# Attention and two MoE layers in one kernel: fewer weights decoded in the first block, zeros stored later, a steeper decode in the second MoE, two steps in another order

## The chip, the core and the metric

The kernel runs on one core of a Trainium2 chip. The metric is the device time of one execution in microseconds (us); lower is better. A core has TensorE (PE, with its weight loads PEld), VectorE (DVE), ScalarE (ACT), GpSimd (POOL) and SyncE (SP). SP computes nothing here: it issues nearly all DMAs of the kernel, in program order, and an instruction of SP that waits holds back every transfer that is written after it.

## The reference

Attention over 4 batches, 8 heads, 576 positions and 64 channels, with a causal mask and a bias that is made from running sums of `s`; then two MoE layers over all 2304 tokens, the second fed with the first one's output.

```
s_pos = np.maximum(s, 0.0)
cum = np.cumsum(s_pos, axis=-1)
bias = -(cum[:, :, :, None] - cum[:, :, None, :])
scores = np.where(causal, -1000000000.0, scores + np.minimum(bias, 0.0))
...
h = np.maximum(x @ w_in, 0.0)           # first MoE
return (h * h @ w_out).astype(np.float32)
...
h = x @ w_in                            # second MoE
g = h * np.cos(h)
return (g @ w_out).astype(np.float32)
```

## The kernel before, in words

**Blocks and jobs.** The 2304 tokens are cut into nine blocks of 256. Attention is computed in jobs: a job is one tile of up to 128 queries of one head. The first 16 heads (numbers 0 to 15, EARLY) are short ones: their keys and queries come by a plain load into a tile `early`, a few heads ahead (`load_raw`), and their scores are turned on PE (line 612). Later heads take `raw` tiles, which ACT and DVE split into `hi` and `k2` (`prep_high`, `prep_low`), and four extra rows that POOL loads from the DRAM table `ext_d`; their scores are turned by DMA transposes that SP issues (line 619).

**Steps.** `step` writes out one step of everything, in program order for each engine: parts of several jobs at different stages (mask, exponential, split, product with v), some slots of the first MoE, and some weights to decode. Each engine runs its own part in that order. A step without MoE slots belongs to the prologue: 21 steps that compute the attention of block 0. Then, for each block k, `moe_slot` hands out the slots of block k's MoE: `g1` (line 943, 12 matmuls that multiply one group f of 128 hidden channels out, for f from 0 to 15) and `g2` (line 972, 12 matmuls back), while the steps go on with the attention of block k+1. The stretch in which block 0's MoE is computed is called block 0 below; it has 17 steps, numbered here 0 to 16, each with about two slots.

**Weights.** The weights come packed as int64 bit patterns of doubles, in 32 pieces of 128x512 for each MoE; piece 2f belongs to `g1` of group f, piece 2f+1 to `g2`. A piece is loaded (`w_load`, line 190, 512 KB), clipped on ACT (`w_clip`, line 805), has its bits put together on DVE in two instructions (`w_bits`, lines 811 and 815), gets its high part from ACT (`w_hi`, line 824) and its low part from DVE (`w_lo`, line 836), and then is a matmul operand. Bits are done in one step, the high and low part in the step after it. How many pieces a step takes comes from constants: with x = step - 4, a prologue step takes int((x+1)*PROLOG_BITS) - int(x*PROLOG_BITS) pieces (PROLOG_BITS is 0.75), a step i of block 0 takes int((i+1)*1.5) - int(i*1.5), until all 32 are done. `w_need` guarantees before each slot that the pieces it uses have been written out; the wait itself is a semaphore on PE. All nine blocks reuse the decoded pieces.

**Other queues.** Work that has no place in a step stands in the list `later`, with the number of a step from which it may go; one entry is taken per step. Among them: `store_ones` at 8 (two DMAs that fill `ext_d` with ones and minus ones), `store_zeros` at 9 (four DMAs of 4x4x64 that put zeros over a part of what the ones filled, for the heads that share a tile, called paired), `pair_mask` at 10 (two small ACT copies), `store_c` at 11. A `store_ext` per unit of eight heads comes 10 jobs ahead of that unit. At the end of a step, `v_late` (the late half of v's preparation, whose last part stores a split v to DRAM, line 480) stands ahead of `heads_ahead(i, (nraw, load_raw, 4))` (the load of a coming head, lines 227 and 232).

**The second MoE.** After the ninth block, 80 steps of three groups p = 0, 1, 2 (`GROUPS`), five token blocks j (four of 512 tokens and a last one of 256, whose steps are half as long on PE) and the groups f. A step is `m2_g1` (line 1372) and, two steps later, `m2_g2` (line 1427). Its weights are decoded in the same way with a scale on top; the number decoded by step i is `goal`, line 1489.

Of the kernel before, what the change touches and what calls it, by code (L numbers as in the profile page):

```python
# [8 lines left out]
F32 = mybir.dt.float32  # L9
# [9 lines left out]
B, H, S, D = 4, 8, 576, 64  # L19
# [4 lines left out]
NF = DFF // 128  # L24
BT = 256
# [66 lines left out]
KQ = 832  # L92


def _paired(head):

    return head[4] == [64]
# [4 lines left out]
    return 128 if _paired(head) else head[6]  # L102

WAHEAD = 8
PROLOG_BITS = 0.75

EARLY = 16
FIRST_BITS = 4
B8_BITS = 0.75
P_BITS = 0.75  # L110
QUIET = 3
PAUSE = 14
# [3 lines left out]
EXT_AHEAD = 10  # L116
# [10 lines left out]
def attention_moe_moe_kernel(  # L127
# [18 lines left out]
    nc = tc.nc  # L146
    ctx.enter_context(tc.manual_schedule())
    heads = _units()
# [15 lines left out]
    ext_d = dram.tile([len(heads), 4, KQ], F32, name="ext_d")  # L164
# [6 lines left out]
    mask = const.tile([128, 768], BF16, name="mask")  # L171
# [26 lines left out]
    one = wp.tile([128, 1024], F32, tag=f"w{2 * NF - 7}", name="one")  # L198
# [36 lines left out]
    def v_own(b):  # L235
# [24 lines left out]
        out=ident, in_=ident, pattern=[[-1, 128]], compare_op=ALU.not_equal, fill=1.0,  # L260
# [23 lines left out]
    def store_ones(eng, n0, n1):  # L284
# [10 lines left out]
        out=mask[:, 384:512], in_=mask[:, 384:512], pattern=[[-1, 128]], compare_op=ALU.is_ge,  # L295
        fill=-8.0e9, base=0, channel_multiplier=1,
    )
    for t in early[2:]:
        early_ones(t, nc.gpsimd)
    nc.vector.tensor_scalar(  # L300
        out=cs[0:32, 0:S], in0=cs[0:32, 0:S], scalar1=0.0, scalar2=8.0, op0=ALU.max, op1=ALU.mult
    )
    cc = []
    for x0, x1, t in ((0, BT, "xh"), (BT, S, "xl")):
        nc.vector.tensor_tensor_scan(
            out=c8[0:32, x0:x1], data0=cs[0:32, x0:x1], data1=cs[0:32, x0:x1],
# [8 lines left out]
    for r in range(2):  # L315
        nc.gpsimd.memset(one[0:len(heads), BT * r:BT + (KQ - BT) * r], 1.0 - 2.0 * r)

    nc.gpsimd.memset(one[0:H // 2, KQ:KQ + 64], 0.0)

    def pair_mask():  # L320
        for r in (0, 64):
            nc.scalar.copy(mask[r:r + 64, 704:768], mask[0:64, 384:448])

    def store_zeros():
        for n in range(EARLY, len(heads), H):
            for x in range(2 if _paired(heads[n]) else 0):
                nc.sync.dma_start(
                    out=ext_d[n + x:n + H:2, :, BT - 64 - 64 * x:BT - 64 * x],
                    in_=one[0:H // 2, None, KQ:KQ + 64].to_broadcast([H // 2, 4, 64]),
                )  # L330

    def split_sums(x0, x1, t):
        c = m1.tile([128, KD * BT], F32R, tag=t, bufs=2, name="cc")
# [5 lines left out]
    def store_ext(n):  # L339
        u, b, h, q0, rws, o, nq, nk, nl = heads[n]  # L340
        src = c_d[b * H:(b + 1) * H]
        nc.sync.dma_start(out=ext_d[n:n + H, 0:2, BT:BT + nl], in_=src[:, :, 0:nl])
        if _paired(heads[n]):
            for x in range(2):
                e = ext_d[n + x:n + H:2]
                nc.sync.dma_start(out=e[:, 2:4, BT - 128 + 64 * x:BT - 64 + 64 * x], in_=src[x::2, :, q0:q0 + nq])
            return
        nc.sync.dma_start(out=ext_d[n:n + H, 2:4, BT - nq:BT], in_=src[:, :, q0:q0 + nq])

# [145 lines left out]
    def v_late():  # L495
        if vq:
            for f, g in vq.pop(0):
                if f not in (v_scale, v_sum):
                    f(g)
# [270 lines left out]
    def job(i):  # L770
        return jobs[i] if 0 <= i < NJ else None
# [7 lines left out]
    def heads_ahead(i, *fs):  # L779
        if job(i) and jobs[i][1] == 0:  # L780
            for cnt, f, d in fs:
                upto(cnt, jobs[i][0] + d, f)

    def unit_done(u):
        return last_job[u] + lag(last_job[u]) + 3
# [197 lines left out]
    def y_store():  # L983
        while yst:
            k, a, st = yst.pop(0)
            nc.sync.dma_start(out=y_d[k, :, 2 * a:2 * a + 2, :], in_=st)
# [59 lines left out]
    seg0 = [n for n in range(NH) if heads[n][2] == 0]  # L1046
    later = []
# [53 lines left out]
    def step(moe=0, bits=0, attn=True):  # L1101

        i = prog[0]
        held = len(xtq)
        prog[0] += attn
        if attn:
            for j in stage(1, i - 2):
                emit_exp(j)
        x_high()
        if attn and job(i - 2):  # L1110
            emit_turn(i - 2)
        if attn:
            heads_ahead(i, (next_, load_ext, 2))
        w_age()
        w_scales()
        n = moe_slot() if moe else None
        slow = bool(vq) and any(f is v_wait for f, g in vq[0])
        if slow:
            v_sums()
        if attn:  # L1120
            heads_ahead(i, (nhigh, prep_high, 2))
        _weave(evacuate())
        y_evict()
        if not attn or g2done[0] < 2:
            rests()
        if xcq and xcq[-1][-1] and xcq[-1][0] == 1:
            x_low()
        _weave(softmax_tail(i) if attn else None, w_step(bits), None if slow else v_early())
        x_low()
        rests()  # L1130
        w_lows()
        if attn and job(i - 1) and jobs[i - 1][0] < EARLY:
            for j in stage(1, i - 1):
                emit_exp(j)
        act(n)
        if attn:
            heads_ahead(i, (nlow, prep_low, 2))
        if slow:
            _weave(v_early())
        if not (attn and last_block(i)):  # L1140
            y_store()
        if attn and job(i):
            emit_qk(i)
        if attn and last_block(i):
            heads_ahead(i, (nraw, load_raw, 4))
        for _ in range(moe - 1):
            act(moe_slot())
            y_evict()
        w_sums()
        if attn:  # L1150
            for j in stage(1, i - 1):
                emit_exp(j)
        behind = any(job(j) and _paired(heads[jobs[j][0]]) for j in (i - 6, i - 5))
        if attn and not behind:
            values(i)
        turn(held if moe and i > last_job[0] + TURN_FROM else len(xtq))
        if not slow:
            v_sums()
        if attn:
            for j in stage(3, i - LAG[0]):  # L1160
                if j > i - lag(j):
                    stages[3] -= 1
                    break
                emit_pv(j)
        if attn and behind:
            values(i)
        p_turn()
        w_ahead()
        v_late()
        if attn:  # L1170
            heads_ahead(i, (nraw, load_raw, 4))
        y_store()
        if later and prog[0] >= later[0][0]:
            later.pop(0)[1]()
# [91 lines left out]
    later.append((4, store_c1))  # L1266
    later.append((6, lambda: v_own(1)))
    later.append((8, lambda: store_ones(nc.sync, EARLY, len(heads))))
    later.append((9, store_zeros))
    later.append((10, pair_mask))  # L1270
    later.append((11, store_c))
    for n in seg0[EARLY // H:]:
        first = next(i for i, j in enumerate(jobs) if j[0] == n)
        later.append((first - EXT_AHEAD, lambda n=n: store_ext(n)))
    while prog[0] < unit_done(0):
        i = prog[0]
        x = i - FIRST_BITS
        step(bits=int((x + 1) * PROLOG_BITS) - int(x * PROLOG_BITS) if x >= 0 else 0)

    for k in range(NB1):  # L1280
        start = prog[0]
        goal = unit_done(k + 1) if k + 1 < NB1 else start
# [6 lines left out]
        for i in range(J):  # L1289
# [25 lines left out]
            n = len(slots) - last - nslots + math.ceil(nslots * (i + 1) / J)  # L1315
# [134 lines left out]
    bits0 = nw[2]  # L1450
    for i in range(len(steps2) + G2LAG):
        new = i < len(steps2)
        if i >= QUIET:
            w_age()
            w_scales()
        if i == 5:
            y_scales(NB2 - 1, NB2)
        if new:
            p, j, f = steps2[i]
            w_stats(2 * NF + 2 * GROUPS[p][1])  # L1460
            w_need(2 * NF + 2 * f + 2)
            m2_g1(j, f)
            m2_cos(j, f)
        if i < G2LAG:
            m2_sin(j, f)
            m2_mul(p, j, f)
            m2_high(p, j, f)
            m2_rest(p, j, f)
        elif i <= len(steps2) and i > G2LAG:
            m2_high(*steps2[i - 1])  # L1470
        if i >= QUIET:
            w_squares()
            while wrest:
                w_rest(wrest.pop(0))
        if new:
            if p == 0 and j + 2 < NB2 and f == 3:
                first_y(j + 2)
            if i >= G2LAG:
                m2_sin(j, f)
        if G2LAG < i <= len(steps2):  # L1480
            m2_rest(*steps2[i - 1])
        if i >= G2LAG:
            m2_g2(*steps2[i - G2LAG])
        if new and p == 0 and j + 1 < NB2 and f == 1:
            last_y(j + 1)
        if new:
            w_lows()
            k = i + 1 - QUIET
            goal = min(4 * NF, bits0 + int(max(0, min(k, PAUSE) + max(0, k - PAUSE - 5)) * P_BITS))
            if i >= QUIET:  # L1490
                _weave(w_step(max(0, goal - nw[2])))
            if i >= G2LAG:
                m2_mul(p, j, f)
            if p == 0 and j + 2 < NB2 and f == 2:
                power_y(j + 2, 0)
            if nw[2] < 4 * NF and i >= QUIET:
                w_ahead()
        if i >= QUIET:
            w_sums()
        if i == 3:  # L1500
            y_sums(NB2 - 1, NB2)
# [49 lines left out]
```

## Time and profile before

| what | value |
|---|---|
| median of 3 runs | 986.95 us (983.54 to 987.28) |
| the profiled execution, its own time | 987.32 us |
| its span | 985.5 us, so 1.8 us lie around it |
| busy, PE / PEld | 956.0 us (97%) / 735.2 us (75%) |
| busy, DVE / ACT / POOL | 716.6 us (73%) / 656.2 us (67%) / 163.3 us (17%) |
| read from and written to HBM | 85.79 MB, 15.83 MB |

PE is busy for 97% of the span, but its share is not even: it is lowest in the first 50 us, the prologue. First MoE and attention end at about 606 us; the rest is the second MoE. The profiled execution is 0.4 us above the median of the runs.

### The profile page before, as it was taken

The numbers are of one execution on the slowest core, as the hardware profiler recorded it, in microseconds if no ns is written. First come the engines' busy times: TensorE is split into PE (matmuls) and PEld (weight loads), VectorE is DVE, ScalarE is ACT, GpSimd is POOL, SyncE is SP. The second block draws the span as 40 slices with busy tenths as digits, with TensorE's granted clock in tenths as the row PEclk, the third lists the DMA queues.
The fourth block names the chain that finished last, engine by engine and source line by source line (L and its number), as shares of the span: only waits on it lengthen the run. The fifth ranks groups of instructions, "written<-read, shape, count | busy, mean of one in ns | idle before, by whom it ended". The sixth has DMA issues, their size and how long they took to land.

```text
span 985.5 us, 20389 instructions
## 1 busy us (share of the span) xinstructions
PE 956.0 (97%) x7250; PEld 735.2 (75%) x7250; DVE 716.6 (73%) x1816; ACT 656.2 (67%) x1596; POOL 163.3 (17%) x252
## 2 busy tenths in 40 slices
PE   5799999999999999999999999999999999999998
PEld 4698999999999999999999997445544454444444
DVE  6779987778778777777997265898778885555555
ACT  6689877877778778676785686677556664334333
POOL 2000011111111111111110022430144430001101
PEclk9999999999999999999999999999999999999999
DMA  8785488656886885477898579200000000001001
GB/s 257 240 257 184 114 200 221 189 138 159 178 181 168 188 200 153 122 150 164 188 223 164 210 261 344 84 22 1 1 1 1 0 1 1 12 32 43 34 10 65
DMA packets 150518, 127.19 MB, mean 129 GB/s; under 512 B 107864, under 2 KB 125600, under 8 KB 150416
## 3 DMA queue, kind: packets, MB, share of 16 engines
q1 hardware_dynamic: 146512, 119.59, 46.1%
q0 software_dynamic: 3904, 6.30, 2.5%
q8 instruction: 57, 0.93, 0.4%
q14 instruction: 45, 0.37, 0.1%
HBM read 85.79 MB, written 15.83 MB: 103 GB/s over the span
## 4 chain that ended last, share of the span: by engine, by line
PE 84%; DVE 5%; ACT 4%; DMA 4%; issue 2%; SPq 1%; POOL 0%; DVEq 0%; ACTq 0%; POOLq 0%
PE hp L1372 19%; PE hps L943 19%; PE y L972 18%; PE o L1427 18%; PE qkp L558 5%; PE pvs L685 4%; DMA rw<-in_w_dram 3%; PE xps L740 1%; DVE wt L836 1%; DVE st L815 1%; DMA early<-in_qk_dram 1%; DMA ext_d<-one 1%; ACT sb L599 1%; ACT st L805 1%; ACT g L955 0%
## 5 line engine op out<-in xcount | busy, mean ns | idle before, releaser
L943 PE MATMUL hps<-xh,wt 128*128 128x256 f32 x1152 | 239.3, 291 | 1.7 <-ACT g L954 1.6
L972 PE MATMUL y<-gh,wt 128*128 128x256 f32 x1152 | 236.5, 288 | 0.0
L943 PEld LDWEIGHTS hps<-xh,wt 128*128 128x128 f32 x1152 | 190.5, 192 | 3.8 <-ACT g L954 2.8
L972 PEld LDWEIGHTS y<-gh,wt 128*128 128x128 f32 x1152 | 188.9, 191 | 1.0
L1372 PE MATMUL hp<-yh,wt 128*128 128x512 f16 (+1 forms) x640 | 185.9, 358 | 0.0
L1427 PE MATMUL o<-wt,gh 128*128 128x512 f16 x576 | 171.4, 379 | 0.6 <-ACT gh L1407 0.5
L943 PE MATMUL hps<-xl,wt 128*128 128x256 f32 x576 | 163.5, 284 | 0.0
L972 PE MATMUL y<-gl,wt 128*128 128x256 f32 x576 | 162.8, 283 | 0.1
L1372 PEld LDWEIGHTS <-wt 128*128 128x128 f16 x960 | 91.9, 98 | 93.0
L1384 ACT ACTIVATE a<-hp,hsc 128x512 f32<-128x512 f32 (+1 forms) x80 | 51.4, 643 | 115.6 <-PE hp L1372 114.2
L954 ACT ACTIVATE g<-hps 128x256 f32<-128x256 f32 x144 | 54.7, 380 | 104.4 <-PE hps L943 103.0
L1372 PE MATMUL hp<-yl,wt 128*128 128x512 f16 (+1 forms) x320 | 114.4, 358 | 0.0
L943 PEld LDWEIGHTS hps<-xl,wt 128*128 128x128 f32 x576 | 111.0, 193 | 0.3
L972 PEld LDWEIGHTS y<-gl,wt 128*128 128x128 f32 x576 | 110.1, 191 | 1.0 <-DVE gl L962 0.4
L1427 PE MATMUL o<-wt,gl 128*128 128x512 f16 x288 | 109.2, 379 | 0.1
L1427 PEld LDWEIGHTS <-gh 128*128 128x128 f16 x576 | 56.2, 98 | 65.3 <-ACT gh L1407 1.4
L1385 DVE TENSOR_SCALAR kf<-a 128x512 f32<-128x512 f32 (+1 forms) x80 | 35.0, 438 | 95.0 <-ACT a L1384 94.5
L384 POOL DMA_DIRECT2D k<-ext_d x80 | 41.2, 516 | 321.0 <-ACT g L955 105.9
L599 ACT ACTIVATE sb<-sb,nb 128x128 f32<-128x128 f32 (+7 forms) x152 | 87.6, 576 | 2.9 <-DVE nb L576 2.8
L962 DVE TENSOR_TENSOR gl<-g,gh 128x256 fp32r<-128x256 f32 x144 | 60.2, 418 | 29.5 <-ACT gh L956 16.3
L1393 ACT ACTIVATE a<-kf 128x512 f32<-128x512 f32 (+1 forms) x80 | 46.8, 585 | 48.2 <-DVE kf L1386 48.0
L576 DVE CUSTOM_DVE_ANT_0 sb<-qkp,mask 128x128 f32<-128x128 f32 (+7 forms) x152 | 69.3, 456 | 13.1 <-PE qkp L543 9.9
(125 smaller groups left out, 1685.4 us busy)
## 6 DMA issues: line engine op xcount, KB each, us to landing
rw<-in_w_dram SPq DMA_DIRECT2D x64, 512.0 KB
raw<-in_qk_dram SPq DMA_DIRECT2D x48, 352.0 KB
raw<-in_qk_dram SPq DMA_DIRECT2D x16, 384.0 KB
v_d<-vt SPq DMA_DIRECT2D x16, 320.0 KB
vb<-v_d SPq DMA_DIRECT2D x32, 160.0 KB
vr<-in_v_dram POOLq DMA_DIRECT2D x15, 320.0 KB, 4.2
y_d<-yst SPq DMA_DIRECT2D x18, 256.0 KB
yr<-y_d SPq DMA_DIRECT2D x9, 512.0 KB
```

The lines of the kernel that those rows point to most:

```text
L384: nc.gpsimd.dma_start(out=hd[n][1][64:68, BT - nq:BT + nl], in_=ext_d[n, :, BT - nq:BT + nl])
L558: nc.tensor.matmul(p[0:r, 0:cn], m[0:kk, qo:qo + r], m[0:kk, BT + c0:BT + c0 + cn], start=(kk == 128 and not (two and h % 2)), stop=(kk == ...
L576: nc.vector.tensor_tensor_reduce(out=sb[0:r, c0:c0 + cn], in0=p[0:r, 0:cn], in1=mask[0:r, mo:mo + cn], scale=-0.125, scalar=(3.0e38 if k = ...
L599: nc.scalar.activation(out=sb[0:r, 0:w], in_=sb[0:r, 0:w], func=ACTF.Exp, scale=-1.0, bias=j["nb"], accum_out=z[0:r, ti, x:x + 1],)
L943: nc.tensor.matmul(hp, w[:, a, c * 128:(c + 1) * 128], (xh, xl)[e][:, c, :], start=(n == 0), stop=(n == 3 * KD - 1),)
L954: nc.scalar.activation(out=g, in_=hp, func=ACTF.Relu)
L962: nc.vector.tensor_tensor(out=gl, in0=g, in1=gh, op=ALU.subtract)
L972: nc.tensor.matmul(yps[k][d // 2][:, d % 2, :], w[:, a, d * 128:(d + 1) * 128], (gh, gl)[e], start=(f == 0 and n == 0 and d % 2 == 0), sto ...
L1372: nc.tensor.matmul(hp, w[:, a, c * 128:(c + 1) * 128], (yh, yl)[e][:, c, :], start=(m == 0), stop=(m == 3 * KD - 1),)
L1384: nc.scalar.activation(out=a, in_=hp, func=ACTF.Copy, scale=sm["hsc"][:, j, f:f + 1], bias=0.25)
L1393: nc.scalar.activation(out=a, in_=kf, func=ACTF.Sin, scale=-6.2831850)
L1427: nc.tensor.matmul(ops[j][a], (gh, gl)[e][:, a * 128:(a + 1) * 128], w[:, x, :], start=(first and m == 0), stop=(last and m == 2),)
```

## The change

Five edits:

1. `PROLOG_BITS` goes from 0.75 to 0.6. In the 17 prologue steps that decode, int(17*0.75) = 12 pieces become int(17*0.6) = 10. Block 0's rate stays, so that it ends its 32 pieces two later.
2. `store_zeros` is gone. The zeros of the paired heads are stored in `store_ext`, beside the unit's sums, from columns of `mask` that hold zeros; the small memset that made the old source is gone too.
3. `pair_mask` moves from step 10 of the prologue to a step 8 jobs ahead of the third unit, which lies in block 0.
4. In a step's end, `heads_ahead` with `load_raw` stands ahead of `v_late`.
5. In the second MoE, `goal` grows by one piece a step, not by 0.75, after a pause.

```diff
-PROLOG_BITS = 0.75
+PROLOG_BITS = 0.6
...
-    nc.gpsimd.memset(one[0:H // 2, KQ:KQ + 64], 0.0)
...
-    def store_zeros():
-        for n in range(EARLY, len(heads), H):
-            for x in range(2 if _paired(heads[n]) else 0):
-                nc.sync.dma_start(
-                    out=ext_d[n + x:n + H:2, :, BT - 64 - 64 * x:BT - 64 * x],
-                    in_=one[0:H // 2, None, KQ:KQ + 64].to_broadcast([H // 2, 4, 64]),
-                )
...
                 nc.sync.dma_start(out=e[:, 2:4, BT - 128 + 64 * x:BT - 64 + 64 * x], in_=src[x::2, :, q0:q0 + nq])
+                nc.sync.dma_start(
+                    out=e[:, :, BT - 64 - 64 * x:BT - 64 * x],
+                    in_=mask[0:H // 2, 0:128].bitcast(F32)[:, None, :].to_broadcast([H // 2, 4, 64]),
+                )
...
         w_ahead()
-        v_late()
         if attn:
             heads_ahead(i, (nraw, load_raw, 4))
+        v_late()
...
-    later.append((9, store_zeros))
-    later.append((10, pair_mask))
...
+        if n == seg0[EARLY // H]:
+            later.append((first - EXT_AHEAD + 2, pair_mask))
...
-            goal = min(4 * NF, bits0 + int(max(0, min(k, PAUSE) + max(0, k - PAUSE - 5)) * P_BITS))
+            goal = min(4 * NF, bits0 + int(max(0, min(k, PAUSE)) * P_BITS) + max(0, k - PAUSE - 5))
```

Three places show what moves. The first is SP's queue in the middle of the prologue; `rw` is a weight piece, `ext_d<-one` are the stores of the ones (80 heads) and of the zeros (4x4x64), and `early` is head number 8. Before:

```order
L190 DMA rw<-in_w_dram 128x1024 x2
L288 DMA ext_d<-one 80x2x256
L288 DMA ext_d<-one 80x2x576
L327 DMA ext_d<-one 4x4x64 x4
L190 DMA rw<-in_w_dram 128x1024 x2
L227 DMA early_343<-in_qk_dram 64x512
L228 DMA early_343<-c_d 2x512
```

and with the change:

```order
L190 DMA rw<-in_w_dram 128x1024
L288 DMA ext_d<-one 80x2x256
L288 DMA ext_d<-one 80x2x576
L190 DMA rw<-in_w_dram 128x1024 x2
L227 DMA early_327<-in_qk_dram 64x512
L228 DMA early_327<-c_d 2x512
```

The four stores of zeros are gone from here, and three pieces, not four, stand ahead of the head's load.

The second place is DVE in steps 13 and 14 of block 0, from the mask of a job (ISA) of step 13 on; `st` is a piece at its bits, `wt<-st` a low part, `p<-sb` the split of a job's weights. Before:

```order
L576 ISA sb,nb<-qkp,mask 128x512
L576 ISA nb 128x1
L811 TENSOR_SCALAR st_1337<-st_1337 128x512
L640 TENSOR_SCALAR p<-sb 128x384
L815 SCALAR_TENSOR_TENSOR st_1337<-rw,st_1337 128x512
L644 SCALAR_TENSOR_TENSOR p<-sb,p 128x384
L962 TENSOR_TENSOR gl<-g,gh 128x256
L836 TENSOR_TENSOR wt<-st,wt 128x512
...
L640 TENSOR_SCALAR p<-sb 128x512
L644 SCALAR_TENSOR_TENSOR p<-sb,p 128x512
L962 TENSOR_TENSOR gl<-g,gh 128x256
L836 TENSOR_TENSOR wt<-st_1337,wt 128x512
```

and with the change:

```order
L570 ISA sb,nb<-qkp,mask 128x512
L570 ISA nb 128x1
L805 TENSOR_SCALAR st<-st 128x512 x2
L634 TENSOR_SCALAR p<-sb 128x384
L809 SCALAR_TENSOR_TENSOR st<-rw,st 128x512 x2
L638 SCALAR_TENSOR_TENSOR p<-sb,p 128x384
L956 TENSOR_TENSOR gl<-g,gh 128x256
L830 TENSOR_TENSOR wt<-st_1261,wt 128x512
...
L809 SCALAR_TENSOR_TENSOR st_1386<-rw,st_1386 128x512
L638 SCALAR_TENSOR_TENSOR p<-sb,p 128x512
L956 TENSOR_TENSOR gl<-g,gh 128x256
L830 TENSOR_TENSOR wt<-st,wt 128x512 x2
```

Before, the low part in the first step is that of piece 30 and the one in the second that of piece 31. With the change they are those of piece 28, and of 29 and 30; piece 31 comes a step later. PE's own order is the same here in both.

The third place is DVE in the second MoE, around the short steps of p = 1, which are the rows with 256 columns. Before:

```order
L864 TENSOR_SCALAR wsm<-stat 128x2
...
L1385 TENSOR_SCALAR kf<-a 128x256
L1386 SCALAR_TENSOR_TENSOR kf<-kf,a 128x256
L839 SCALAR_TENSOR_TENSOR wt_12047<-st,wsc,wt_12047 128x512
L839 SCALAR_TENSOR_TENSOR wt_12049<-st,wsc,wt_12049 128x512
L1399 SCALAR_TENSOR_TENSOR a<-hp_12027,gsc,a 128x256
```

and with the change:

```order
L833 SCALAR_TENSOR_TENSOR wt_11894<-st,wsc,wt_11894 128x512
L833 SCALAR_TENSOR_TENSOR wt_11896<-st,wsc,wt_11896 128x512
L1393 SCALAR_TENSOR_TENSOR a<-hp_11874,gsc,a 128x512
L1379 TENSOR_SCALAR kf<-a 128x512
L1380 SCALAR_TENSOR_TENSOR kf<-kf,a 128x512
L1393 SCALAR_TENSOR_TENSOR a<-hp_11916,gsc,a 128x512
L1379 TENSOR_SCALAR kf<-a 128x256
```

The last two low parts stood among the short steps; with the change they stand two full steps ahead of the first short one.

## Rows read from the trace of the kernel before

**Rows 1.** Stretches: length; busy us of PE, PEld, DVE, ACT, POOL; clock, DMA, GB/s.

```profile
75.00:100.00 25.00, 22.80 (x188) 22.21 (x187) 23.05 (x62) 23.35 (x61) 2.05 (x3) 1.00 0.54 181
100.00:125.00 25.00, 23.82 (x196) 23.07 (x195) 22.65 (x58) 22.47 (x59) 2.30 (x4) 1.00 0.50 129
125.00:150.00 25.00, 24.53 (x253) 23.31 (x252) 21.83 (x59) 19.79 (x53) 3.55 (x6) 1.00 0.82 203
150.00:200.00 50.00, 48.42 (x518) 45.89 (x517) 38.91 (x118) 38.82 (x111) 8.60 (x19) 1.00 0.78 200
```

**Rows 2.** Chain of waits, first 130 us (start us, us, what); `...` stands for left-out lines.

```profile
26.75 6.77 DMA ext_d<-one
...
52.32 2.56 PE hps L943 x12
...
55.74 2.21 PE hps L943 x12
...
115.25 1.45 PE hps L943 x12
```

**Rows 3.** SP's timeline (start us, us, engine line op tiles, count).

```profile
33.57 1.27 SPq L327 DMA_DIRECT2D ext_d<-one  x4
34.88 0.83 SPq L190 DMA_DIRECT2D rw<-in_w_dram  x2
35.76 0.51 SPq L227 DMA_DIRECT2D early<-in_qk_dram  x1
```

**Rows 4.** What SP waited for in the first 130 us (us, times, longest).

```profile
SPq L327 <- DMA ext_d<-one: 5.5, 1, 5.5
...
SPq L480 <- DVE vt L473: 3.6, 1, 3.6
```

**Rows 5.** Timelines of PE and of DVE (in brackets: idle before it, releaser).

```profile
42.74 0.77 PE L543 MATMUL qkp<-early 66*128 66x128 f32 x2 [5.53 <-DMA early<-in_qk_dram]
...
43.54 0.29 DVE L576 CUSTOM_DVE_ANT_0 sb<-qkp,mask 128x128 f32<-128x128 f32 x1 [4.31 <-PE qkp L543]
```

**Rows 6.** Stretches of 4 us, columns as in rows 1.

```profile
28.00:32.00 4.00, 3.60 (x16) 3.13 (x15) 3.97 (x14) 2.89 (x10) 0.00 (x0) 1.00 0.87 280
32.00:36.00 4.00, 3.91 (x16) 2.96 (x15) 3.80 (x12) 3.60 (x10) 0.00 (x0) 1.00 0.29 77
36.00:40.00 4.00, 1.21 (x5) 0.91 (x5) 3.19 (x10) 2.43 (x7) 0.00 (x0) 1.00 0.80 265
...
44.00:48.00 4.00, 4.00 (x18) 3.69 (x18) 3.16 (x10) 3.29 (x9) 0.00 (x0) 1.00 0.97 298
```

**Rows 7.** One piece's three DVE instructions (DVE's timeline), and the two mask copies (ACT's timeline).

```profile
28.36 0.42 DVE L811 TENSOR_SCALAR st<-st 128x512 int32<-128x512 int32 x1
28.81 0.69 DVE L815 SCALAR_TENSOR_TENSOR st<-rw,st 128x512 int32<-128x512 int32 x1
29.42 0.69 DVE L836 TENSOR_TENSOR wt<-xst,wt 128x512 fp32r<-128x512 f32 x1
...
25.38 0.49 ACT L322 COPY mask<-mask 64x64 bf16<-64x64 bf16 x2
```

**Rows 8.** First matmuls of g1 for f = 13, 14 and 15 (PE's timeline).

```profile
103.85 0.29 PE L943 MATMUL hps<-xh,wt 128*128 128x256 f32 x1
...
107.29 0.28 PE L943 MATMUL hps<-xh,wt 128*128 128x256 f32 x1
...
111.05 0.29 PE L943 MATMUL hps<-xh,wt 128*128 128x256 f32 x1
```

**Rows 9.** Low parts in steps 12, 13 and 14 of block 0 (DVE's timeline).

```profile
105.54 1.29 DVE L836 TENSOR_TENSOR wt<-st,wt 128x512 fp32r<-128x512 f32 x2
...
110.29 0.69 DVE L836 TENSOR_TENSOR wt<-st,wt 128x512 fp32r<-128x512 f32 x1
...
114.76 0.69 DVE L836 TENSOR_TENSOR wt<-st,wt 128x512 fp32r<-128x512 f32 x1
```

**Rows 10.** PE's only idle time of 800 to 825 us (PE's timeline).

```profile
813.60 0.60 PE L1427 MATMUL o<-wt,gh 128*128 128x512 f16 x2 [0.49 <-ACT gh L1407]
```

## Prediction

> **What bounds the kernel now.** I read the longer stretches first. PE idles 1.2 us in 100 to 125 us, 0.5 us in 125 to 150 and 1.6 us in 150 to 200 [rows 1]; from there it is busy to the end but for single gaps. So TensorE's work sets the time after block 0, and what can still move is the first 125 us. There the chain of waits was read next. It runs through the store of the ones (6.77 us from issue to landing) and comes to PE's first MoE group at 52.32 us [rows 2]. SP's timeline shows why: after the two stores of ones it issues nothing until 33.57 us, when the first store of zeros goes out, which overwrites a part of what the ones wrote and waits for them to land, 5.5 us [rows 2, 3, 4]. Everything behind it on SP waits too: two weight pieces and then the load of head 8, at 35.76 us [rows 3]. That load comes late: PE stands idle for 5.53 us and DVE for 4.31 us, until 42.74 and 43.54 us [rows 5]. Meanwhile the DMA engines run dry: their busy share falls to 0.29 in 32 to 36 us [rows 6].
>
> Up to there, and again from about 60 us, DVE is the pace: 3.97 of 4 us in 28 to 32 us [rows 6], 23.05 and 22.65 of 25 us in block 0, with ACT at 23.35 and 22.47 and PE at 22.80 and 23.82 [rows 1]. These three are nearly balanced, and decoding is what fills DVE and ACT.
>
> **The change, part by part. Zeros out of the prologue.** SP's wait goes. The head's load can then be issued about 6.9 us earlier: right behind the ones at 28.0 us (33.57 less the 5.5 of waiting) plus two weight issues of 0.83 us, so at 28.9 and not 35.76 [rows 3, 4]. That is the upper end of the gain. It does not land so much earlier, because the ones and the weights ahead of it still have to be moved. By the transfers: the idle shares of three 4 us stretches are 0.13, 0.71 and 0.20, so 4.2 us of DMA time come free [rows 6], and one weight piece fewer stands ahead of the load, 512 KB at 298 GB/s or 1.8 us [rows 6]. 42.74 less 6.0 is 36.7 us. I take 6.0: a landing waits for transfers, not for an issue. The lower end is the hole alone, 4.2. PE itself does not stand in the way: it wanted the head at 42.74 - 5.53 = 37.2 us, and with two pieces fewer decoded by then it wants it at about 34. From there to block 0 both kernels decode three pieces, so block 0 begins **6.0 us earlier** (4.2 to 6.9).
>
> **Two pieces fewer in the prologue.** One piece costs DVE 0.45 + 0.61 + 0.60 = 1.66 us from start to start [rows 7], two cost 3.3. In the prologue the saving is hidden: PE would still wait for head 8, from 34 to 36.7. In block 0 the pieces come back, and they come at its end: steps 0 to 12 decode as many as before, with the same work, but each step holds pieces with a number lower by two. What stands against this is PE's order, which has not moved. It begins g1 of f = 13, 14 and 15 at 103.85, 107.29 and 111.05 us [rows 8] and needs the low parts of pieces 26, 28 and 30. Before, these were done in steps 10, 12 and 13; with the change in steps 12, 13 and 14. I read their time from the low parts that stand in those steps now [rows 9], in the clock of before:
>
> Piece 26 takes the place at 105.54 and is done at 105.54 + 0.69 = 106.2; PE is ready at 103.85 and waits 2.4 us. Piece 28 takes the place at 110.29, behind one more pair of bit instructions (1.06 us [rows 7]), so it is done at 112.0; PE would be ready at 107.29 + 2.4 = 109.7 and waits 2.3. Piece 30 takes the place at 114.76, behind two more pairs (2.1) and behind piece 29 (0.6), done at 118.2; PE would be ready at 111.05 + 4.7 and waits 2.4. Together PE loses 7.1 us, because it runs ahead of DVE here and had up to a step in hand. The bounds are 3.3, DVE's own added work, and 7.1. I take **7.1**, since DVE has no idle time in those steps that could absorb it, and both engines start 6.0 earlier alike.
>
> **What comes back.** PE reaches the end of block 0 later relative to DVE than it does now, so the waits that it has behind that, 0.5 + 1.6 us [rows 1], mostly vanish: -1.8, bounds 0 and -2.1.
>
> **The mask copies.** They are 0.49 us on ACT [rows 7], now in block 0, where ACT is nearly full: +0.3, bounds 0 and 0.5. The zeros' four stores move beside other stores of `ext_d`; at 1.27 us for four issues [rows 3] they delay SP by 0.6 us for each of two units, ten jobs ahead of their reader and with the DMA transposes next behind them, whose result PE uses several steps later. I cost them at nothing; without that cover they would cost 1.3.
>
> **Raw loads ahead of v's store.** SP's longest wait in a store of v is 3.6 us [rows 4], and a raw load now passes it; the store is pushed back by one issue. PE waits for neither. 0, bounds -0.5 and +0.5.
>
> **Second MoE.** The last pieces' high and low parts fall into the short steps, and PE idles there once, 0.49 us, for ACT [rows 10]. With decoding done ahead of the short steps, as DVE's order shows, this goes: -0.5, bounds 0 and -0.5. The faster rate could only cost where DVE or ACT fill up, and PE has no other gap there.
>
> **Sum**: -6.0 + 7.1 - 1.8 + 0.3 - 0.5 = -0.9 us against the profiled execution's 987.3, so 986.4. That execution is 0.4 above the median of 986.95; as a median the forecast is **986.0 us**, no change that shows. About 0.5% (4.9 us) is what a measurement of this kernel tells from no change: below 982.0 is faster, above 991.9 slower.
>
> **The rivals.** *PE keeps its lead* (0.20). If DVE comes into steps 12 to 14 less far behind than I read, the three waits shrink to DVE's own 3.3 us or to nothing, with no waits recovered behind them: -6.0 + 3.3 + 0.3 - 0.5 = -2.9 to -6.2, so 984.0 to 980.7. For it: piece 30's low part ended at 110.98 and g1 began at 111.05, so the schedule was tight already and cost PE nothing [rows 8, 9]. Against it: the low parts are written a step later, and DVE is full.
>
> *The transfers hold the gain to the hole* (0.13). If the landing moves only by the DMA engines' idle time, block 0 begins 4.2 us earlier: 986.0 + 1.8 = 987.8. For it: the share is about full on both sides of the hole [rows 6]. Against it: one piece fewer stands ahead. [...]
>
> *TensorE's clock is up sooner* (0.10). PE's first two groups take 2.56 and 2.21 us, a later one 1.45, which is the lower against the upper of its two levels although the clock column reads 1.00 [rows 2, 6]. With the hole in the prologue gone the clock could be up at block 0's start: 2 x 1.45 for 4.77, so -1.9, and 984.1. Against it: PE was busy for 4.00 of 4 us in 44 to 48 us [rows 6] and the groups at 52 us were still slow. [...]
>
> *The clock falls in block 0* (0.05, the slower side). The place is PE's three new waits of 2.3 to 2.4 us. The longest idle time that it has here now is part of the 2.2 us in 75 to 100 us [rows 1], and the groups behind it run at 1.45 [rows 2]. If a wait is long enough to drop the clock, it may stay down as it did from 42.74 to the second group's end near 57.2 us, 14.5 us of half speed with PE busy; half of that is lost: +7.2, so 993.2.
>
> **How the numbers follow.** The forecast has 0.50, the rivals 0.48, and 0.02 is left. Faster by over 0.5% needs the better half of the first rival, or the clock on top of bounds that all fall well: 0.20. Slower is the clock's fall and little else: 0.06. The rest, 0.74, is within 0.5%. The range, 980.8 to 988.6, takes in the first rival to its end, the clock's rise and the transfers' case, and leaves out the clock's fall.
>
> **What would show it.** Right: no wait of SP behind the ones; PE's wait for head 8 down to some 3 us and ended near 36.7; the first g1 near 46 us; then three new waits of PE at line 937 (g1's line after the change) for low parts of DVE, 6 to 7 us in all, between about 97 and 113 us; fewer PE waits from 125 to 200; no gap near 810. Wrong: no such waits of PE (then the time is near 982), a first g1 at 50 us or later, or groups of 12 matmuls at 2.5 us past block 0's start.

## The result and the profile after

The changed kernel takes 990.98 us (median of 10 runs, 988.15 to 993.66) against 986.41 us of the kernel before (10 runs, 982.88 to 987.63): the ratio is 1.0051, with a 95% interval of 1.0037 to 1.0065. It is slower by about 4.6 us, where I had forecast 986.0 and no change that shows, with 988.6 as the upper end of the range. A later set of runs gave 990.94 us and the same 1.0051 (1.0036 to 1.0066).

The page of the kernel after: PE's busy time has grown by 4.9 us, from 956.0, with the same 7250 matmuls, and the clock row, which read 9 in all forty slices before, shows a 7 in the fifth (98.9 to 123.6 us).

```profile
PE 960.9 (97%) x7250; PEld 739.7 (75%) x7250; DVE 715.0 (72%) x1816; ACT 656.3 (66%) x1596; POOL 163.5 (17%) x251
...
PEclk9999799999999999999999999999999999999999
```

Stretches of the kernel after (columns as in [rows 1]; the number behind POOL's is the granted clock as a share of full speed):

```profile
75.00:100.00 25.00, 21.40 (x161) 20.09 (x160) 23.43 (x60) 21.92 (x58) 2.01 (x3) 0.96 0.48 160
100.00:125.00 25.00, 20.04 (x116) 18.98 (x116) 15.48 (x38) 14.80 (x37) 0.67 (x2) 0.77 0.36 89
125.00:150.00 25.00, 24.53 (x254) 23.39 (x253) 20.98 (x56) 21.46 (x56) 2.63 (x5) 1.00 0.86 184
150.00:200.00 50.00, 48.61 (x503) 46.19 (x502) 39.30 (x116) 37.52 (x105) 9.12 (x19) 1.00 0.86 203
```

Against [rows 1], 100 to 125 us holds 116 matmuls, not 196; DVE and ACT are down to 15.5 and 14.8 of 25 us, so neither is the pace there. Behind 125 us PE's busy share and clock are as before.

The beginning went as forecast, and a little better. SP's queue in the kernel after, and the chain of waits of the same stretch:

```profile
24.29 0.92 SPq L288 DMA_DIRECT2D ext_d<-one  x2
25.25 2.15 SPq L190 DMA_DIRECT2D rw<-in_w_dram  x2
27.45 0.68 SPq L227 DMA_DIRECT2D early<-in_qk_dram  x1
```

```profile
27.45 8.98 DMA early<-in_qk_dram
...
36.57 0.77 PE qkp L537 x2
...
45.43 2.00 PE hps L937 x12
...
47.90 1.70 PE hps L937 x12
...
50.06 1.47 PE hps L937 x11
```

SP no longer stands behind the ones [rows 3, 4]. Head 8's load is issued at 27.45 and not 35.76, takes 8.98 us, and PE begins with the head at 36.57 and not 42.74 [rows 5]. The first two groups of `g1` take 2.00 and 1.70 us where they took 2.56 and 2.21 [rows 2], and the third is at full speed (1.47 us): the clock is up sooner. The clock column reads 1.00 there in both kernels, so this is read from the matmuls: one that takes `xl` lasts 0.41 us up to the one at 57.03 us before and at 46.08 us after, and 0.28 us behind it. In block 0 of the kernel after it lasts 0.41 us where the column reads 0.50 and 0.28 us where it reads 1.00. In the run with 0.7 (Experiments) the column itself reads 0.50 in 32 to 48 us.

The end of block 0 took all of it back. PE's timeline, the places where it waits at `g1` of f = 13, 14 and 15 (in brackets the idle time before, and what ended it):

```profile
95.66 0.39 PE L937 MATMUL hps<-xh,wt 128*128 128x256 f32 x1 [0.81 <-ACT wt L818]
...
97.11 0.50 PE L937 MATMUL hps<-xh,wt 128*128 128x256 f32 x2 [0.95 <-DVE wt L830]
...
103.69 0.38 PE L937 MATMUL hps<-xh,wt 128*128 128x256 f32 x1 [1.59 <-ACT wt L818]
...
105.47 0.80 PE L937 MATMUL hps<-xh,wt 128*128 128x256 f32 x2 [1.29 <-DVE wt L830]
...
114.16 0.51 PE L937 MATMUL hps<-xh,wt 128*128 128x256 f32 x2 [1.97 <-DVE wt L830]
```

Those are the three waits of the forecast, 6.6 us in all (0.81 + 0.95, 1.59 + 1.29 and 1.97). What I had given a chance of 0.05, a fall of TensorE's clock, came with them. Stretches of 2 us of the kernel after:

```profile
97.00:99.00 2.00, 1.89 (x12) 1.89 (x12) 2.00 (x5) 0.00 (x0) 0.00 (x0) 0.70 0.06 20
99.00:101.00 2.00, 2.00 (x12) 2.00 (x11) 0.19 (x2) 1.85 (x6) 0.77 (x1) 0.50 0.67 200
...
107.00:109.00 2.00, 2.00 (x11) 2.00 (x11) 0.24 (x1) 0.92 (x3) 0.00 (x0) 0.50 0.86 245
109.00:111.00 2.00, 2.00 (x12) 2.00 (x11) 1.06 (x5) 2.00 (x6) 0.00 (x0) 0.50 0.05 17
...
115.00:117.00 2.00, 2.00 (x12) 2.00 (x11) 0.00 (x0) 0.81 (x3) 0.00 (x0) 0.50 0.10 21
```

Behind each of the three waits the granted clock falls to 0.50, the lower of the two levels that the column shows (of the 160 stretches of 0.5 us between 50 and 130 us, 130 read 1.00, 24 read 0.50, and the six in which it changes lie between): 11 or 12 matmuls in 2 us, where the kernel before has 17 to 19 in those stretches of block 0 in which PE is as busy.

Since PE's order has not moved, the same matmul can be looked up in both traces, and the difference of its starts (called the lag below; negative is earlier than before) says where time went. Each column is one profiled execution, and how far such lags scatter is told in the section on the prediction:

| matmul | before | after | difference |
|---|---|---|---|
| first of head 8 | 42.74 | 36.57 | -6.17 |
| third group of `g1` | 58.41 | 50.06 | -8.34 |
| last ahead of `g1` for f = 13 | 103.62 | 94.45 | -9.17 |
| last ahead of the group behind f = 15 | 114.91 | 118.82 | +3.91 |
| in block 1 | 199.63 | 203.55 | +3.92 |
| first MoE, near its end | 583.45 | 588.52 | +5.07 |
| second MoE, behind its short steps | 832.49 | 836.03 | +3.54 |
| near the end | 977.63 | 981.18 | +3.55 |

So 9.2 us are won ahead of f = 13, and 13.1 are lost in the next 24 us. The same 87 matmuls in both traces, first the kernel before, then after:

```profile
103.62:114.75 11.13, 10.74 (x87) 10.41 (x86) 10.85 (x28) 10.13 (x27) 1.79 (x3) 1.00 0.56 160
```

```profile
94.45:118.64 24.19, 17.57 (x87) 16.12 (x85) 14.54 (x35) 12.38 (x30) 1.77 (x3) 0.72 0.32 86
```

PE is busy 6.8 us longer with the same work, by the clock, and idle 6.6 us, not 0.4. That is a sum of two, but not yet two causes: a slower PE may only have filled time in which it would have waited.

### The profile page after: what moved, and what is told of

Same layout as the page of the kernel before. It is cut to its first block, busy times and chain, and to the rows that moved or that the text cites. A ratio compares the mean times of both kernels' runs of the same rounds, so it can differ in the third digit from the quotient of the medians.

```text
span 989.1 us, 20373 instructions
## 1 busy us (share of the span) xinstructions
PE 960.9 (97%) x7250; PEld 739.7 (75%) x7250; DVE 715.0 (72%) x1816; ACT 656.3 (66%) x1596; POOL 163.5 (17%) x251
## 4 chain that ended last, share of the span: by engine, by line
PE 83%; DMA 6%; DVE 5%; ACT 3%; issue 1%; SPq 1%; DVEq 0%; POOL 0%; ACTq 0%; POOLq 0%
PE hp L1366 19%; PE hps L937 19%; PE o L1421 19%; PE y L966 17%; PE qkp L552 4%; PE pvs L679 4%; DMA rw<-in_w_dram 2%; DMA early<-in_qk_dram 2%; DMA raw<-in_qk_dram 1%; DMA pt<-p 1%; PE xps L734 1%; DVE wt L830 1%; DVE st L809 1%; SPq L190 1%; ACT sb L593 0%
## 5 line engine op out<-in xcount | busy, mean ns | idle before, releaser
L966 PE MATMUL y<-gh,wt 128*128 128x256 f32 x1152 | 239.4, 291 | 0.0
L966 PEld LDWEIGHTS y<-gh,wt 128*128 128x128 f32 x1152 | 191.5, 193 | 1.0
```

The source lines that it names most:

```text
L966: nc.tensor.matmul(yps[k][d // 2][:, d % 2, :], w[:, a, d * 128:(d + 1) * 128], (gh, gl)[e], start=(f == 0 and n == 0 and d % 2 == 0), sto ...
```

## Experiments

Each run is given with its median, and with its ratio to the kernel before on the same chip (medians 985.74, 986.11 and 985.63 us in the three sets). All lags below are starts of the same matmul in a run's trace and in that of the kernel before, as in the table.

**Is it the two pieces?** The changed kernel with edit 1 undone:

```diff
-PROLOG_BITS = 0.6
+PROLOG_BITS = 0.75
```

> The changed kernel with PROLOG_BITS back at 0.75, all else as changed. Theory A (the two pieces decoded later cost block 0 its end: PE's waits for w26, w28, w30 and the clock that fell in them, 13.1 us between the same matmuls in the traces): those waits and the fall of the clock go, block 0 still begins 5 to 6.5 us earlier than before, the first groups of 12 matmuls still find the clock up sooner (-2), and the 1.4 us that came back in the second MoE's neighbourhood stay: 977.5 to 981, point 979. The granted clock of 97 to 118 us reads 1.00. Theory B (the loss is that everything runs earlier, or the moved zeros, mask copies and loads, and not the number of pieces): the waits of PE at line 937 stay, the time is 986 or more.

Measured: 980.89 us, 0.9951 (0.9934 to 0.9968). Theory A holds: no wait at line 937 for a low part, and the four other edits together are worth 4.9 us. Edit 1 on top of them costs 10 us (1.0051 against 0.9951), twice what the whole change lost. The granted clock reads 1.00 in 94 to 119 us; it did fall once in this profile, at 83 us, behind a wait that other kernels have too (last section).

**Edit 1 alone**, on the kernel before:

```diff
-PROLOG_BITS = 0.75
+PROLOG_BITS = 0.6
```

> The kernel before with PROLOG_BITS at 0.6 and nothing else: SP's wait for the ones stays. Theory A: head 8 comes at most 1.8 us earlier (one piece of 512 KB less ahead of it), the clock is as late as before, and block 0's end loses about 13 us: 994 to 1000, point 997, with the granted clock at 0.5 in parts of the last 25 us of block 0. Theory B (the waits come from an earlier block 0): 984 to 988 and no such waits.

Measured: 991.25 us, 1.0059 (1.0040 to 1.0078), slower as theory A says but by half of what I expected, and the reason is in the prologue. SP's and PE's timelines of this run:

```profile
25.84 0.92 SPq L288 DMA_DIRECT2D ext_d<-one  x2
...
31.19 1.35 SPq L327 DMA_DIRECT2D ext_d<-one  x4
...
32.99 0.74 SPq L227 DMA_DIRECT2D early<-in_qk_dram  x1
...
37.29 0.77 PE L543 MATMUL qkp<-early 66*128 66x128 f32 x2 [3.29 <-DMA early<-in_qk_dram]
```

The zeros still wait for the ones, but go at 31.19 and not 33.57, and head 8 comes to PE at 37.29 and not 42.74, 5.45 us sooner, half of it because its load is issued at 32.99 and not 35.76, the other half because it takes 4.3 us from issue to use and not 7.0. One piece fewer stands ahead of it on SP. So in this profile edit 1 by itself wins nearly as much as moving the zeros does (5.70, next run), and the two do not add: both together brought 6.17. In block 0 it then loses nearly what the change loses: the lag goes from -8.71 at 88 us to +3.05 in `g1` of f = 15 and +2.55 behind it, where the change went from -9.17 to +3.91.

**The zeros and the mask copies alone** (edits 2 and 3 on the kernel before, as in the change's diff):

> The kernel before with the zeros' stores and the mask copies moved as in the change and nothing else: after_p75 without the reordered raw load and without the steeper goal of the second MoE. Theory A: the early part as in after_p75, and only the 0.97 us gap near 812 us and the small shifts at 234, 242 and 596 us differ: 978.5 to 982, within 1.5 us of after_p75. Theory B, if the reordered load is what makes PE wait in block 0: this one is over 4 us faster than after_p75.

Measured: 984.54 us, 0.9982 (0.9970 to 0.9994). The profiled execution shows the early part as expected (head 8 at 37.03, a lag of -5.7 that stays about -5 to the end), but it is one of the fastest of twelve, which spread from 981.1 to 986.6. By medians this is 3.7 us slower than the change without edit 1, which has all four other edits. Neither expectation holds: the first had it within 1.5 us of that kernel, the second over 4 us faster. The two edits that it lacks, the order of the raw load and the goal, were tried singly.

```diff
-        v_late()
         if attn:
             heads_ahead(i, (nraw, load_raw, 4))
+        v_late()
```

> The kernel before with the raw load ahead of v's store and nothing else. By the trace (lags of 0.5 and 0.4 us at 234 and 242 us that came with the whole change): within 1 us of before, 985 to 987. If this edit is what sets after_p75 3.6 us below the kernel with the zeros alone: 983 to 984.

```diff
-            goal = min(4 * NF, bits0 + int(max(0, min(k, PAUSE) + max(0, k - PAUSE - 5)) * P_BITS))
+            goal = min(4 * NF, bits0 + int(max(0, min(k, PAUSE)) * P_BITS) + max(0, k - PAUSE - 5))
```

> The kernel before with the steeper goal of the second MoE and nothing else. By the trace the gap at 813.6 us and a second one behind it go, 0.97 us: 984.3 to 985.3 beside 985.7 of before. If this edit carries what after_p75 has over the kernel with the zeros alone: 982 to 983.5.

Measured: 984.47 us, 0.9982 (0.9971 to 0.9993), for the raw load, and 985.46 us, 0.9989 (0.9975 to 1.0004), for the goal. Neither expectation of the first is right: it gains some 1.6 us by medians. Its profile has a lag of -0.85 at head 8, near 42 us, but SP's order first differs from before at 81 us, so that this part isn't the edit's; from there to the end the lag only goes from -1.2 to -1.24. How the edit gains, and whether it does beyond scatter, stays open. The second shows its gap gone (the lag moves by 0.7 us at 813.6 us and by 0.3 just behind), and its median agrees with the expected 1 us, but its interval takes in no change. Together they make 2.3 us, of the 3.7 that were to be explained; the rest is not shown to be more than noise, since each of these ratios is known to 0.1 or 0.2% (1 to 2 us).

**One piece fewer**, as a dose, with 0.7 in place of 0.6:

> The changed kernel with PROLOG_BITS at 0.7: 11 pieces in the prologue, one fewer than before. w26 and w30 come a step later than before, w28 in the same step; with 0.6 all three are late, w26 by two steps. If the loss follows the steps in which the pieces come: two waits of PE in place of three, a shorter fall of the clock: 3 to 7 us over the 980.9 of 0.75, 984 to 988, point 985. If PE has a step in hand: no waits, 979 to 982.

Measured: 987.47 us, 1.0009 (0.9996 to 1.0021), some 6 us over 0.75 by the ratios: the first expectation by its time, not by its waits. PE waits ahead of one group only, that of f = 15, 1.29 us for ACT and then 3.46 us for DVE's low part, and the clock falls there too (0.50 in 110 to 115 us):

```profile
106.31 0.38 PE L937 MATMUL hps<-xh,wt 128*128 128x256 f32 x1 [1.29 <-ACT wt L818]
...
110.28 0.80 PE L937 MATMUL hps<-xh,wt 128*128 128x256 f32 x2 [3.46 <-DVE wt L830]
```

Piece 26 came a step later too and cost nothing. So a step late is not a wait each time: here PE still had a lead at f = 13 and none left at f = 15.

**What the clock costs by itself.** In the changed kernel PE was given other work where it waited: extra matmuls on pieces long decoded, which the real group's first matmul overwrites, so that the output is the same.

```diff
+FILL = {-3: 12, -2: 18, -1: 12}
...
+        if k == 0 and f >= NF - 3:
+            for m in range(FILL[f - NF]):
+                nc.tensor.matmul(
+                    hp, wt[0, 0, 0][:, 0, m % KD * 128:(m % KD + 1) * 128], xh[:, m % KD, :],
+                    start=(m == 0), stop=(m == FILL[f - NF] - 1),
+                )
```

> The changed kernel with 12, 18 and 12 extra matmuls of 256 columns on PE ahead of g1 of f = 13, 14 and 15 in block 0, whose result the first real matmul overwrites: PE works where it waited, 1.4 to 2.2 us each at the upper clock. If the clock's fall costs by itself (6.8 us more of busy PE for the same 87 matmuls): the granted clock stays at 1.00 and 3 to 7 us come back, 984 to 988. If PE's slower matmuls were hidden, because DVE and ACT set these steps anyway: 990 to 992, with the clock at 1.00 and longer waits after the extra matmuls. If the clock falls although PE works there: 0.5 in the column, 991 or more.

Measured: 989.34 us, 1.0030 (1.0015 to 1.0044). It falls between the first two expectations: waits of 0.5 to 1.7 us were left, and the clock fell once, to 0.50 in 107 to 109 us. So more of them, 17, 32 and 26, beside the changed kernel itself on the same chip:

> The changed kernel as it is, on the chip of the three runs beside it: 990 to 992 by its first ten runs, 4 to 6 us slower than before. If the verdict of those runs was chance: within 2 us of before.

> As after_fill with 17, 32 and 26 extra matmuls, by the waits that were left in its trace (0.6, 1.8 and 1.7 us): PE should have no wait of over 0.5 us before g1 of f = 13 to 15 and the granted clock read 1.00 to 125 us. If the clock's fall is half of the loss, as the busy time of the 87 matmuls says (17.57 against 10.74 us), and PE's speed counts because ACT and DVE wait for PE's results in turn: 984.5 to 987.5, 4 to 6 us below after_again. If PE's slower matmuls are hidden behind DVE: within 1.5 us of after_again.

Measured: 990.94 us, 1.0051 (1.0036 to 1.0066), and 988.32 us, 1.0029 (1.0015 to 1.0044). PE's timeline of the second (line 938 are the extra matmuls, line 944 is `g1`), and the stretch of the table above:

```profile
95.72 2.20 PE L938 MATMUL hps<-xh,wt 128*128 128x256 f32 x17
...
101.45 4.00 PE L938 MATMUL hps<-xh,wt 128*128 128x256 f32 x32
...
106.07 0.50 PE L944 MATMUL hps<-xh,wt 128*128 128x256 f32 x2 [0.39 <-DVE wt L831]
...
109.69 3.28 PE L938 MATMUL hps<-xh,wt 128*128 128x256 f32 x26
...
113.70 0.50 PE L944 MATMUL hps<-xh,wt 128*128 128x256 f32 x2 [0.49 <-DVE wt L831]
```

```profile
94.45:118.64 24.19, 23.31 (x186) 22.53 (x185) 16.47 (x40) 14.40 (x34) 1.78 (x3) 1.00 0.32 86
```

The clock stays at 1.00 to 125 us, and 2.6 us come back by the medians, neither 4 to 6 nor less than 1.5; the two intervals just overlap, so the size rests on the traces. In the lags, from the matmul ahead of f = 13 to the one behind f = 15, the changed kernel loses 13.3 us on this chip (-8.83 to +4.47), this one 10.0 (-8.13 to +1.90). So the clock's fall is worth about 3 us of the 13, and 10 are waiting, even with PE at full speed: 2.20 + 4.00 + 3.28 us of extra matmuls and 0.88 of waits behind them make 10.4.

**Making the two pieces up early**, on the changed kernel:

```diff
-                bits = int((i + 1) * B0_BITS) - int(i * B0_BITS)
+                bits = int((i + 1) * B0_BITS) - int(i * B0_BITS) + (i in (1, 3))
```

> The changed kernel with one more piece in each of steps 1 and 3 of block 0, so that the two pieces are made up at once; from there on every piece is done in the step in which the kernel before had it. If the loss comes from the pieces being late at the end of block 0: no waits of PE for DVE's low parts at f = 13 to 15, the granted clock stays at 1.00, and the early gain stays, since DVE is busy for only 4.5 of 8 us in 44 to 52 us of the changed kernel: 977.5 to 981, point 979, and 11 to 13 us faster than the change. If fewer pieces in the prologue cost by themselves, wherever they are made up (DVE is full all along, or the weights come late): 984 or more, with waits of PE earlier in block 0.

Measured: 985.15 us, 0.9983 (0.9970 to 0.9996). The waits at f = 13 to 15 are gone, and some 6.7 us with them by the ratios, not 11 to 13: the lag goes from -9.17 at 58 us to -3.75 ahead of f = 13. Steps 1 and 3 now take three pieces, and PE stands still behind the second (PE's timeline, then DVE's), with the clock down behind that wait (0.89 in the mean of 60 to 75 us; a matmul of line 937 that takes `xl` lasts 0.28 us at 65.92 and 0.42 us at 66.36 us):

```profile
65.06 0.18 PE L437 MATMUL xps<-ss,ones 128*128 128x2 bf16 x1 [3.68 <-DVE xl L751]
...
62.24 0.43 DVE L805 TENSOR_SCALAR st<-st 128x512 int32<-128x512 int32 x1 [2.19 <-ACT st L799]
```

The same with the two in steps 0 and 2, `(i in (0, 2))`, so that no step takes more than two:

> The changed kernel with one more piece in each of steps 0 and 2 of block 0 (two pieces in each of its first four steps; with the extra ones in steps 1 and 3 these had three, and PE stood for 3.68 us behind the second of them). If it is the step with three pieces that cost after_catch its start: no wait of over 1.5 us in 50 to 90 us, no fall of the clock, 978 to 982, point 980. If two pieces more in the first steps overrun PE's lead however they are spread: 983 to 986.

Measured: 981.83 us, 0.9961 (0.9948 to 0.9974), as the first expectation says of the time; the wait at this place is 1.1 us. Two of its signs failed: PE waits for 1.68 us near 81 us, and the clock falls behind that wait (last section). And with 0.7 and one more piece in step 0:

> The changed kernel with 11 pieces in the prologue (PROLOG_BITS 0.7) and one more in step 0 of block 0, so that no piece is later than before. If the whole loss of after_p70 is the one wait of 4 us for w30's low part and the clock that falls in it: that wait goes, and 979 to 982 is left, as with 0.75. If fewer pieces in the prologue cost on their own: 984 or more.

Measured: 980.79 us, 0.9950 (0.9938 to 0.9962), the first expectation. This and the change without edit 1 (0.9951) are the fastest, 0.5% below the kernel before, and the two can't be told apart: a prologue with fewer pieces costs nothing that shows by itself, if none of them is later than PE's order wants it.

## Why the prediction was wrong

**Zeros out of the prologue, -6.0: right, at -6.17.** Landing 36.43 forecast as 36.7, PE's wait 2.55 us forecast as some 3. The load was issued 8.31 us sooner and came to PE 6.17 us sooner, so that the landing followed the issue only in part, as I had argued for this load. One trace fixes this only loosely: the six traces whose prologue is the same (the change, its repeat, the two with extra matmuls and the two with extra pieces in block 0) have head 8 earlier by 4.87 to 7.94 us, 6.2 in the mean. The two terms of the 6.0 were wrong, 4.2 for the hole behind the ones and 1.8 for the piece fewer: the zeros alone bring 5.70, edit 1 alone 5.45. They overlap, so that the whole came out right by luck.

**The clock up sooner, a rival at 0.10: came.** The lag grows from -6.17 to -8.34 through the first groups, 2.2 us where I had priced 1.9. It also comes with edit 1 alone (-5.45 to -7.25), only by 0.9 us in the change without edit 1 (-5.83 to -6.72), and not in the profile of the zeros alone (-5.70 to -5.73), so it is not the hole in the prologue that decides it, as the rival had it. It goes rather with the pieces, though the ranges overlap: in the seven traces with 0.6 the first matmul at full speed comes 1.2 to 3.6 us behind the first of `g1`, in the seven with 0.7 or 0.75 it is 2.0 to 5.4. PE is also busier earlier in those with 0.6, 4.00 of 4 us in 24 to 28 us in all seven, against 3.14 to 3.93. Why the clock rises sooner there was not tested and stays open. Without this rise the forecast would have missed by 2.2 us more.

**Two pieces fewer, +7.1: the step that failed. It was +13.1**, some 10 of it waiting and 3 the clock. The three waits stand where they were forecast, for the pieces that were forecast. Their size was taken "in the clock of before", with "no idle time" in DVE, as if it went on at its own pace while PE waits. It does not. The chain of waits of the kernel after, one turn of it:

```profile
97.11 1.95 PE hps L937 x10
...
99.09 0.39 ACT g L948
...
100.97 1.13 ACT st L799 x2
...
102.81 1.20 DVE st L809 x2
...
104.81 0.61 DVE wt L830
...
105.47 2.52 PE hps L937 x10
```

ACT's next clip of weights (line 799) stands in its queue behind the activation of the very group that PE was late with (line 948). DVE's next bits wait for that clip, and PE's next group waits for DVE's low part. Once PE has lost its lead, the three engines go round one after another; a turn takes 8.4 us, and beside it little is done but PE's `g2`. DVE, that I had called full, stands idle, and so does ACT (ACT's timeline, then DVE's):

```profile
99.09 0.38 ACT L948 ACTIVATE g<-hps 128x256 f32<-128x256 f32 x1 [2.70 <-PE hps L937]
...
101.56 0.99 DVE L805 TENSOR_SCALAR st<-st 128x512 int32<-128x512 int32 x2 [2.36 <-ACT st L799]
```

With the clock held up, the waits come to 10 us by the extra matmuls that fitted into them, not 7.1; the first is 2.2 us, near the 2.4 forecast, the second and third some 4 where I had 2.3 and 2.4. I put these 3 us down to the turn, by the chain above; no run changes the order of ACT's queue, so that is read and not tested. That the waits of the changed kernel add up to 6.6 us, near 7.1, is luck: PE at half speed fills the rest.

**The clock's fall in block 0, 0.05: came**, in the three places named. Its price was 7.2 us and the busy time has grown by 6.8, but only about 3 of them are lost: the rest would have been waited. (By [rows 2] the second group ends at 57.95 us, not 57.2, which would have made the price 7.6.) The chance was wrong because I argued from "the longest idle time that it has here now" and the one fast group behind it, though I forecast three waits of 2.4 us close together, of which the trace of before has no like.

**What comes back, -1.8: didn't come.** PE waits for 1.86 us in 125 to 200 us, and 2.05 before [rows 1]; the lag is 3.9 us from 119 to 200 us. The same waits stand in both traces: 0.5 and 0.4 us for ACT's `g`, 0.5 for DVE, and 0.4 without a releaser; only one of 0.2 for DVE is gone.

**Second MoE, -0.5: right in place, -1.0 in size**, beyond its bound of -0.5. The lag drops by 0.66 us at 813.6 [rows 10], as forecast, and by 0.31 just behind, which the forecast didn't have.

**The mask copies and the raw loads** have no place of their own in the traces; the raw load alone seems to gain 1.6 us by medians, where I had 0 with bounds of 0.5, and no trace shows by what.

By the sum: -6.2 in the prologue, -2.2 by the clock and -0.8 until f = 13, then +13.1, 1.2 more by 583 us and -1.5 behind it make +3.6, the difference of the spans (989.1 and 985.5). The -0.8 and the 1.2 are not explained.

## What to carry to other kernels

When work is put off that another engine feeds on, look up by how many steps each item is late at its reader, and follow the ring of queues that the wait closes. Here the reader's result stood ahead of the producer's next input on a third engine, a lead once lost turned into alternation, and the price of a late item was the part of a turn that the reader couldn't fill (some 4 us of 8.4), not the producer's own work (1.7 us a piece). A late item cost nothing while a lead was left (piece 26 with 0.7), so put the postponed work back where the producer idles, spread so that no step grows past its neighbours. And two gains that freed the same transfer did not add (5.70 and 5.45 us alone, 6.17 together): measure each alone and both together before summing.

## What the runs showed of the hardware that I had not expected

TensorE's clock fell behind waits that were neither long nor certain to make it fall. In the kernel after it fell behind waits of 0.81 and 0.95 us with two matmuls between them. In the second profile of that kernel it did the same behind waits of the same two lengths. A wait for ACT at line 606, between 80 and 84 us, is 1.67 or 1.68 us long in five runs. These

```profile
82.17 0.33 PE L606 MATMUL qkp<-ident,sb 128*128 128x128 f32 x1 [1.67 <-ACT sb L593]
```

```profile
83.00:85.00 2.00, 2.00 (x12) 2.00 (x12) 1.46 (x7) 2.00 (x4) 0.00 (x0) 0.56 1.04 417
```

are the change without edit 1, where the clock fell to half right behind it, and these

```profile
80.81 0.33 PE L606 MATMUL qkp<-ident,sb 128*128 128x128 f32 x1 [1.68 <-ACT sb L593]
```

```profile
82.00:84.00 2.00, 2.00 (x11) 2.00 (x10) 1.45 (x6) 2.00 (x4) 0.00 (x0) 0.50 1.03 417
```

are the two more pieces in steps 0 and 2, where it fell too. This

```profile
83.15 0.33 PE L606 MATMUL qkp<-ident,sb 128*128 128x128 f32 x1 [1.67 <-ACT sb L593]
```

is the zeros alone, where all of 75 to 100 us reads 1.00, as it does with 0.7; with 0.7 and one more piece the mean of the whole run is 1.000. Equal waits, then, had two outcomes, twice a fall and three times none, and no run here shows what decides between them.
